# A third of the gate and value products of the last two units, from 28 half-block matmuls to 49 quarter-block matmuls

## Chip, cores and metric

One NeuronCore of one Trainium2 chip runs the whole program; the other seven stand idle. The metric is the device time of one execution in microseconds (us), the median of several. Engines are named as in the profile: PE is TensorE's matmul stream and PEld its weight loads, DVE is VectorE, ACT is ScalarE, POOL is GpSimd, SP is SyncE, which here issues nearly all DMAs.

## What is computed

Retention over 8 batches and 8 heads of 576 positions and 64 channels, then a gated feed-forward layer over the 4608 tokens that come out of it, all in float32:

```python
ret = scale * (q @ k.T) * Dmat                 # Dmat: decay gamma**(i-j), causal
x   = (ret @ v)                                # (8, 576, 8*64) -> (4608, 512)
xn  = x / sqrt(mean(x*x, -1) + 1e-6) * rms_g
g   = xn @ w_gate                              # 512 -> 1536
out = (g / (1 + exp(-g)) * (xn @ w_val)) @ w_out   # 1536 -> 512
```

## The kernel before, in words

**Units.** The tokens are cut into nine units of 512 tokens, numbered 0 to 8 in the code (`u`). Retention makes the rows of x for a unit; the feed-forward part then works on one unit at a time. Units 0 and 1 run in a first stage that also rounds the weights and builds their block sums (a written plan of steps sets its order). Units 2 to 8 run in the loop at L1342 to L1380. Retention for later units is worked in between the groups of units 2 to 6; units 7 and 8 have none beside them.

**Seven products for eight.** Every matrix product of units 2 to 8 is done by a Strassen-Winograd scheme: both operands are cut 2 x 2, seven block products replace eight, and sums of blocks are formed before (of x and of the weights) and after (of the results). `sums_of_x` (L615) makes the sums of x once per unit, `sums` and `t_of[u]` hold them. The seven weight blocks of each group lie ready in DRAM (`w_up_blocks`), as do those of the output weights (`w_out_blocks`).

**Gate and value groups.** `up(u, n)` (L697) makes one group n = 0 to 5; groups with even n are gates (`m` = 0), those with odd n the values that multiply them. Each block product is 256 x 256 by 256 tokens: four matmuls of 128 x 128 weights against 256 moving columns (L706), accumulated in one PSUM bank. A group is 28 matmuls and four banks (`x`, `y`, `z`, `w`). After a product an ACT copy (L732) or a DVE addition (L713) takes its bank; ACT then applies Silu (L727), or DVE multiplies into the gates (L725), and `differences` (L785) prepares operands of the output product.

**Output products.** `across(u)` (L843) multiplies the 1536 hidden rows by `w_out` with the scheme nested twice: 7 x 7 = 49 products of quarters, three matmuls each (one for each 128 rows of the contraction), 128 moving columns, 147 matmuls per unit (L876). `inner_sums` (L821) forms the four inner sums for each of the seven pieces, mostly on POOL; results gather in `vec`, the front part of the tile `vi`; the last step, `combine` (L1065), is seven additions of 128 x 4 x 128 on POOL. `store` (L1078) writes them out with eight DMAs of 128 KB.

**Weights on their way.** Each group's and each output piece's blocks pass through `ring`, a room of 17408 words per partition (L125). `pieces` lists them in order of use with their places (L640 on); a group takes 3584 words (1.84 MB), an output piece 2688 (1.38 MB). `refill` (L656) issues the next loads on SP's queue as soon as the place is free, and is called by `used` (L686) when the products of a piece have been issued. SP works strictly in order; a DMA that waits for room holds everything behind it.

**Order around the change.** The loop is a schedule by hand: each `yield` in `up` and `across` marks a product, and the loop places other work by (group, product):

```python
if n == 1 and i == 4:              # L1349
    store(u - 1)
if n == 2 * NG - 2 and i == 1:     # L1351: group 4
    inner_sums(u, 0, 0)
    inner_sums(u, 1, 0)
if more and i == 2 and 0 < n <= NHP:
    prepare(j0 + n); fetch(j0 + n + 1)   # retention: transposes, next loads
```

So on SP's queue the stores of unit u-1 stand in group 1 of unit u, behind the first `fetch` of that unit and before the other ones. `combine` of unit u-1 is issued at the end of `across(u - 1)`. The eight PSUM banks go round in order of use.

Of the kernel before, what the change touches and what calls it, by code (L numbers as in the profile page):

```python
# [10 lines left out]
F32 = mybir.dt.float32  # L11
U32 = mybir.dt.uint32
AF = mybir.ActivationFunctionType
# [31 lines left out]
def kernel(  # L45
# [32 lines left out]
    assert S == U + L and NU == B + 1 and NK == 3 and NG == 3  # L78

    const = ctx.enter_context(tc.tile_pool(name="const", bufs=1))  # L80
    raw = ctx.enter_context(tc.tile_pool(name="raw", bufs=1))
    att = ctx.enter_context(tc.tile_pool(name="att", bufs=2))
    xp = ctx.enter_context(tc.tile_pool(name="xp", bufs=3))
    tmp = ctx.enter_context(tc.tile_pool(name="tmp", bufs=4))
    PS = bass.MemoryType.PSUM
    dram = ctx.enter_context(tc.tile_pool(name="dram", bufs=1, space=bass.MemoryType.DRAM))
    banks = ctx.enter_context(tc.tile_pool(name="banks", bufs=8, space=PS))

    def bank(name):
        return banks.tile([P, 512], F32, tag="b", name=name)  # L90
# [4 lines left out]
    def row(name):  # L95
        return tmp.tile([P, U], F32, tag="n", name=name, bufs=3)
# [447 lines left out]
    def same_rows():  # L544

        t = tmp.tile([P, SQ], F32, tag="d", name="d", bufs=1)
        nc.vector.tensor_reduce(
            out=t, in_=ident.rearrange("p (a b) -> p b a", b=SQ), axis=mybir.AxisListType.X,
            op=ALU.add,
        )  # L550
        nc.vector.tensor_copy(
            out=alike.rearrange("p (a b) -> p a b", b=SQ),
            in_=t.unsqueeze(1).to_broadcast([P, P // SQ, SQ]),
        )
# [73 lines left out]

    UP, OUT = 7 * 2 * 2 * P, 7 * NK * P
    w_up_d = dram.tile([2 * NG, P, UP], F32, name="w_up_blocks")
    w_out_d = dram.tile([7, NK, P, 7 * P], F32, name="w_out_blocks")
    FIRST_ORDER = (A11, S4, A12, S1, S2, S3, A22)
# [7 lines left out]
    pieces = [("out", 0, n) for n in range(7)] + [("out", 1, n) for n in range(4, 7)]  # L642
    N_FIRST = len(pieces)
    for u in range(2, NU):
        pieces += [("up", u, n) for n in range(2 * NG)] + [("out", u, n) for n in range(7)]
    places = []
    at = AT_SUMS
    for kind, u, n in pieces:
        size = UP if kind == "up" else OUT
        if at + size > RING:  # L650
            at = AT_SETS if kind == "out" and u < 2 else 0
        places.append((at, at + size))
        at += size
    n_sent = n_used = 0

    def refill(most=len(pieces)):  # L656

        nonlocal n_sent
        while n_sent < min(most, len(pieces)):
            a, z = places[n_sent]  # L660
            kind, u, n = pieces[n_sent]
            if any(a < y and x < z for x, y in places[n_used:n_sent]):
                return
            if u > 1 and n_used < N_FIRST and a < NF * U:
                return
            o = ring[:, a:z]
            if kind == "up":
                src = w_up_d[n]
            else:
                o = o.rearrange("p (c x) -> p c x", c=NK)  # L670
                src = w_out_d[order_of(u)[n]].rearrange("c p x -> p c x")
            nc.sync.dma_start(out=o, in_=src)
            n_sent += 1

    def piece(kind, u, n):
        if kind == "out" and u == 1 and n < 4:
            i = pieces.index(("out", 0, n + 3))
        else:
            i = pieces.index((kind, u, n))
        assert i < n_sent and (i == n_used or kind == "out" and u == 0)  # L680
        a, z = places[i]
        if kind == "up":
            return ring[:, a:z].rearrange("p (b c f) -> p b c f", b=7, c=2)
        return ring[:, a:z].rearrange("p (c n d) -> p n c d", n=7, c=NK)

    def used():  # L686
# [10 lines left out]
    def up(u, n):  # L697


        m, f = n % 2, n // 2 * 2  # L700
        w = piece("up", u, n)

        def product(blk, ps, start):
            for i in range(2):
                for c in range(2):
                    nc.tensor.matmul(  # L706
                        ps[:, i * HU : i * HU + HU], lhsT=w[:, PLACE[blk], c, i * P : i * P + P],
                        rhs=t_of[u][blk][:, c], start=(start and i == c == 0), stop=False,
                        skip_group_check=True,
                    )  # L710

        def add(o, a, ps):
            nc.vector.tensor_tensor(out=o, in0=a, in1=pairs_of(ps), op=ALU.add)  # L713

        def result(f, t, nm, a, ps):

            o = h[:, f : f + 2, t * HU : t * HU + HU]
            c = pairs_of(ps)
            if a is not None:
                c = o  # L720
                if m:
                    c = pairs_of(temp(f"{nm}_{u}_{n}")) if nm == "c12" else a
                add(c, a, ps)
            if m:
                nc.vector.tensor_tensor(out=o, in0=o, in1=c, op=ALU.mult)  # L725
            else:
                nc.scalar.activation(out=o, in_=c, func=AF.Silu)  # L727

        x_, y, z, w_ = (bank(f"{nm}_{u}_{n}") for nm in "xyzw")
        s1, u2, u4 = (pairs_of(temp(f"{nm}_{u}_{n}")) for nm in ("m1", "u2", "u4"))  # L730
        product(A11, x_, True)
        nc.scalar.copy(out=s1, in_=pairs_of(x_))  # L732
        yield
        product(S2, y, True)
        add(u2, s1, y)
        yield
        product(S1, z, True)
        add(u4, u2, z)
        yield
        product(A12, x_, False)  # L740
        result(f, 0, "c11", None, x_)
        yield
        product(S3, w_, True)
        result(f + NH, 1, "c22", u4, w_)
        yield
        product(S4, z, False)
        result(f, 1, "c12", u2, z)
        yield
        product(A22, w_, False)
        used()  # L750
        result(f + NH, 0, "c21", u2, w_)
        if m:
            differences(u, f)
        yield

    def up_plain(u, k, n):
# [28 lines left out]
    def differences(u, f):  # L785

        hh = h_1 if u == 1 else h
        b11, b12, b22 = hh[:, f : f + 2, :HU], hh[:, f : f + 2, HU:], hh[:, NH + f : NH + f + 2, HU:]
        for o, a, b in ((t1_of(u)[:, f : f + 2], b12, b11), (b12, b22, b12)):
            nc.vector.tensor_tensor(out=o, in0=a, in1=b, op=ALU.subtract)  # L790
# [52 lines left out]
    def across(u):  # L843
# [148 lines left out]
        for n, nm in enumerate(banks_in_turn):  # L992
# [66 lines left out]
                if n in ahead:  # L1059
                    inner_sums(u, ahead[n])  # L1060
            yield
        if u and not last:
            combine(slice(0, 4), nc.gpsimd)

    def combine(b, eng=nc.vector, late=False):  # L1065

        t = vec[:, b] if isinstance(b, slice) else vec[:, b : b + 1]
        for o, x, y in (
            (A12, A11, A12), (A11, A11, S2), (S1, A11, S1), (S4, S1, S4), (A11, A11, S3),
            (S3, S1, S3), (A22, A11, A22),  # L1070
        ):
            eng.tensor_tensor(out=t[:, :, o], in0=t[:, :, x], in1=t[:, :, y], op=ALU.add)  # L1072
        if late:
            store(NU - 1, b)

# [263 lines left out]

    with tc.manual_schedule():  # L1342
        start()
        for u in range(2, NU):
            j0 = NHP * (u + 1)
            more = u + 1 < B
            for n in range(2 * NG):
                for i, _ in enumerate(up(u, n)):
                    if n == 1 and i == 4:  # L1349
                        store(u - 1)  # L1350
                    if n == 2 * NG - 2 and i == 1:  # L1351
                        inner_sums(u, 0, 0)
                        inner_sums(u, 1, 0)
                    if more and i == 2 and 0 < n <= NHP:
                        if j0 + n < len(jobs):
                            prepare(j0 + n)
                            fetch(j0 + n + 1)
                    if u + 1 < NU and n == 2 * NG - 1:
                        if i < NHP:
                            gather(u + 1, i, square(u + 1, i))  # L1360
                        elif i == NHP:
                            fold(u + 1)
                        elif i == 6:
                            meet(u + 1)
                    if (u, n, i) == (2, 2, 1):
                        same_rows()
                    if more and (n, i) == (NHP, 5) and j0 + NHP == len(jobs):
                        values(j0 + NHP - 1)
                if more and n <= NHP and (n or u == 2):
                    if j0 + n < len(jobs):  # L1370
                        slot(j0 + n, rest=(n > 0))
                    else:
                        carried(j0 + n - 1)
            for i, _ in enumerate(across(u)):
                if u + 1 == NU:
                    continue
                if i == 2:
                    root(u + 1)
                elif i in (3, 4, 5, 6):
                    scale_x(u + 1, (i - 3,))  # L1380
                elif i == 8:
                    sums_of_x(u + 1)
# [27 lines left out]
```

## Time and profile before

| | us |
|---|---|
| median of 3 executions (1100.55 to 1248.33) | 1101.38 |
| the profiled execution | 1099.84 |
| its span, first to last instruction | 1098.0 |
| granted TensorE clock over the span | 0.997 |
| unit 7, first gate matmul to the first of unit 8 | 882.6 to 988.2 |
| six gate and value groups of unit 7 | 72.5 |
| output products of unit 7 | 32.9 |

The profile gives, for each engine, the time in which it was busy and the number of instruction records; a float32 matmul leaves two records. The chain of work is followed back from the last instruction, at each step to what released it. A group of instructions is named by line, engine, operation and the tiles it writes and reads. A timeline lists instructions by start; in it, equal neighbours are merged (x8 is eight records) and lengths of matmuls overlap, since they are pipelined. A window view gives each engine's busy time in a stretch, then the clock, the share of the 16 DMA engines and GB/s. In units 2 to 5, which have retention beside them, a unit takes 115 to 116 us; DMA moves 220 to 250 GB/s there. In unit 7 it moves 214 GB/s, in unit 8 150.

### The profile page before, as it was taken

How to read it: one execution, taken by the hardware profiler on the slowest of the kernel's cores; microseconds unless marked ns; L12 is line 12 of the kernel's file. 1: busy time of each engine (PE TensorE's matmuls, PEld its weight loads, DVE VectorE, ACT ScalarE, POOL GpSimd, SP SyncE). 2: the span in 40 equal slices, each digit the busy share in tenths (PEclk: the TensorE clock that was granted, in tenths of full speed). 3: DMA queues.
4: the chain of work that ended last, by engine and by line, in shares of the span. 5: the costliest groups of instructions: out<-in, count | busy, mean ns of one | idle time of the engine just before them, and what ended most of it. 6: DMA issues, size and time to landing. Idle time of an engine off the chain costs nothing.

```text
span 1098.0 us, 24349 instructions
## 1 busy us (share of the span) xinstructions
PE 1085.8 (99%) x10006; PEld 911.3 (83%) x10006; DVE 729.9 (66%) x1299; ACT 328.2 (30%) x739; POOL 443.8 (40%) x421
## 2 busy tenths in 40 slices
PE   8899999999999999999999999999999999999998
PEld 7654444479988899889988998899888988998898
DVE  3778568877866774677667855677565735674467
ACT  6754565331123412332034203330233111201110
POOL 0026325538430195027702571238321932383236
PEclk9899999999999999999999999999999999999999
DMA  8847776696978876787678875988475755575471
GB/s 215 191 151 254 284 249 205 213 338 193 289 279 227 196 287 223 187 233 245 249 212 200 292 260 148 250 247 293 140 199 198 281 192 175 194 282 163 148 251 40
DMA packets 253871, 243.60 MB, mean 222 GB/s; under 512 B 193216, under 2 KB 213824, under 8 KB 247616
## 3 DMA queue, kind: packets, MB, share of 16 engines
q1 hardware_dynamic: 252320, 241.64, 69.8%
q8 instruction: 79, 1.29, 0.5%
q10 hardware_dynamic: 1440, 0.40, 0.2%
q14 instruction: 32, 0.26, 0.1%
HBM read 211.92 MB, written 30.08 MB: 220 GB/s over the span
## 4 chain that ended last, share of the span: by engine, by line
PE 97%; DVE 1%; ACT 1%; issue 1%; POOL 0%; POOLq 0%; DVEq 0%; ACTq 0%
PE up L766 15%; PE x L706 14%; PE w L706 13%; PE z L706 13%; PE y L706 7%; PE xo L876 6%; PE xp L876 4%; PE zo L876 4%; PE zp L876 3%; PE wo L876 2%; PE yo L876 2%; PE av L386 2%; PE wp L876 2%; PE av L406 2%; PE s L295 2%; PE yp L876 2%
## 5 line engine op out<-in xcount | busy, mean ns | idle before, releaser
L766 PE MATMUL up<-x,ring 128*128 128x512 f32 x384 | 167.1, 594 | 0.0
L706 PE MATMUL x<-x,ring 128*128 128x256 f32 x672 | 161.0, 382 | 0.0
L706 PE MATMUL w<-sums,ring 128*128 128x256 f32 x672 | 158.8, 379 | 0.0
L706 PE MATMUL z<-x,ring 128*128 128x256 f32 x672 | 158.7, 379 | 0.0
L828 POOL TENSOR_TENSOR vi<-h 128x384 f32<-128x384 f32 x32 | 42.4, 1327 | 274.2 <-DVE h L725 264.7
L766 PEld LDWEIGHTS up<-x,ring 128*128 128x128 f32 x384 | 72.2, 190 | 89.4 <-issue 85.1
L706 PEld LDWEIGHTS z<-x,ring 128*128 128x128 f32 x672 | 127.7, 190 | 17.4
L706 PEld LDWEIGHTS w<-sums,ring 128*128 128x128 f32 x672 | 127.6, 190 | 17.4
L706 PEld LDWEIGHTS x<-x,ring 128*128 128x128 f32 x672 | 125.3, 190 | 17.5 <-ACT m L732 0.2
L833 POOL TENSOR_TENSOR vi<-h 128x384 f32<-128x384 f32 (+2 forms) x46 | 43.9, 954 | 148.9 <-DVE h L725 148.9
L1072 POOL TENSOR_TENSOR vi<-vi 128x512 f32<-128x512 f32 (+1 forms) x77 | 78.2, 1029 | 52.0 <-DVE vi L903 35.5
L706 PE MATMUL y<-sums,ring 128*128 128x256 f32 x336 | 79.4, 379 | 0.0
L732 ACT COPY m<-x 128x512 f32<-128x512 f32 x42 | 24.6, 586 | 173.5 <-PE x L706 173.5
L713 DVE TENSOR_TENSOR h<-u,w 128x512 f32<-128x512 f32 x42 | 28.9, 687 | 67.7 <-PE w L706 67.7
L706 PEld LDWEIGHTS y<-sums,ring 128*128 128x128 f32 x336 | 63.8, 190 | 8.7
L713 DVE TENSOR_TENSOR u<-m,y 128x512 f32<-128x512 f32 x42 | 28.8, 685 | 59.9 <-PE y L706 59.3
L727 ACT ACTIVATE h<-h 128x512 f32<-128x512 f32 x63 | 39.7, 630 | 83.4 <-DVE h L713 83.4
L1192 POOL TENSOR_TENSOR vi<-vi 128x512 f32<-128x512 f32 (+1 forms) x24 | 40.7, 1697 | 30.7 <-DVE vi L1181 17.6
L713 DVE TENSOR_TENSOR u<-u,z 128x512 f32<-128x512 f32 x42 | 28.9, 687 | 32.7 <-PE z L706 32.6
L1192 POOL TENSOR_TENSOR ring<-ring 128x512 f32<-128x512 f32 x24 | 30.4, 1273 | 49.2 <-DMA w_up_blocks<-ring 43.7
L333 DVE SCALAR_TENSOR_TENSOR ret<-s,causal 128x256 f32<-128x256 f32 (+2 forms) x112 | 32.0, 336 | 22.3 <-PE s L295 22.3
L430 ACT COPY x<-av 128x192 f32<-128x192 f32 (+6 forms) x136 | 37.8, 278 | 27.9 <-PE av L406 26.5
(327 smaller groups left out, 2055.4 us busy)
## 6 DMA issues: line engine op xcount, KB each, us to landing
ring<-w_out_blocks SPq DMA_DIRECT2D x59, 1344.0 KB, 6.9
ring<-w_up_blocks SPq DMA_DIRECT2D x42, 1792.0 KB, 7.5
w_out_blocks<-vi SPq DMA_DIRECT2D x21, 448.0 KB, 6.3
out_dram<-vi SPq DMA_DIRECT2D x64, 128.0 KB, 3.0
qraw<-in_q_dram SPq DMA_DIRECT2D x96, 72.0 KB, 4.8
kraw<-in_k_dram SPq DMA_DIRECT2D x96, 72.0 KB, 2.6
k<-in_k_dram SPq DMA_DIRECT2D x48, 128.0 KB, 2.8
v<-in_v_dram SPq DMA_DIRECT2D x48, 128.0 KB, 2.8
```

What stands on the lines that cost most here:

```text
L333: nc.vector.scalar_tensor_tensor(out=ret[:p, e, a:z], in0=s[e][:p, a * L : z * L].rearrange("p (c k) -> p c k", k=L), scalar=float(_gamma( ...
L430: nc.scalar.copy(out=o, in_=part)
L706: nc.tensor.matmul(ps[:, i * HU : i * HU + HU], lhsT=w[:, PLACE[blk], c, i * P : i * P + P], rhs=t_of[u][blk][:, c], start=(start and i == ...
L713: nc.vector.tensor_tensor(out=o, in0=a, in1=pairs_of(ps), op=ALU.add)
L727: nc.scalar.activation(out=o, in_=c, func=AF.Silu)
L732: nc.scalar.copy(out=s1, in_=pairs_of(x_))
L766: nc.tensor.matmul(ps, lhsT=w[:, PLACE[blk], c % 2, i * P : i * P + P], rhs=x_of[u][:, c], start=(c == 0), stop=(c == NHP - 1),)
L828: eng.tensor_tensor(out=i1, in0=x12, in1=x11, op=ALU.subtract)
L833: eng.tensor_tensor(out=o[:, c], in0=a[:, c], in1=b[:, c], op=op)
L876: nc.tensor.matmul(ps, lhsT=lhs[:, c], rhs=w[:, s, c], start=((nm, s // 4) not in first), stop=False, skip_group_check=True,)
L1072: eng.tensor_tensor(out=t[:, :, o], in0=t[:, :, x], in1=t[:, :, y], op=ALU.add)
L1192: nc.gpsimd.tensor_tensor(out=t[o], in0=t[x], in1=t[y], op=op)
```

## The change

Three things change. First, in units 7 and 8 the groups 1, 2 and 3 (of 0 to 5) are made by a new function, `up_deep`, with the scheme nested twice, as the output products have it: each of the seven blocks is cut 2 x 2 again, so a group is 49 matmuls of 128 x 128 by 128 columns, in eight PSUM banks. The weight blocks' inner sums are made once, on POOL, by `inner_blocks` in units 3, 4 and 5 (group 1, 2 and 3 in turn), from the ring, and stored in DRAM by seven DMAs of 256 KB each. The ring takes each such group as two pieces (four blocks and three), old blocks and new sums side by side, 7168 words instead of 3584, by three DMAs a piece. The inner sums of x are made on DVE at the start of units 7 and 8 (`inner_x`). The results are summed on POOL (`combine_in`, seven additions of 128 x 4 x 128 a group) and finished (Silu, multiplication, differences) during the next group. The pools of the retention part are closed in unit 7 to make room.

Second, in units 3, 4 and 5 the stores of the unit before move from group 1 to the sixth group, behind the last retention loads of the unit; in units 7 and 8 to group 2. Third, `combine` of the unit before moves, for those units, from the end of `across` into the first group of the next unit: behind `inner_blocks`, or behind the second part of `inner_x`. In units 7 and 8 the two early inner sums move from group 4 to group 5.

```diff
+    HALVES = (0, 4), (4, 7)
+    DEEP = range(1, 4)
+    LATE = (NU - 2, NU - 1)
+    USED_IN = (A11, S2, S1, S3), (A12, S4, A22)
...
-        pieces += [("up", u, n) for n in range(2 * NG)] + [("out", u, n) for n in range(7)]
+        for n in range(2 * NG):
+            if u in LATE and n in DEEP:
+                pieces += [("in", u, (n, i)) for i in range(2)]
+            else:
+                pieces.append(("up", u, n))
+        pieces += [("out", u, n) for n in range(7)]
...
+            elif kind == "in":
+                i, z = HALVES[n[1]]
+                o = o.rearrange("p (b k x) -> p b k x", k=2, x=4 * P)
+                src = w_up_d[n[0]].rearrange("p (b x) -> p b x", b=7)
+                for x, y in spans_of(IN_ORDER[i:z]):
+                    nc.sync.dma_start(
+                        out=o[:, x : x + len(y), 0], in_=src[:, y[0] : y[0] + len(y)]
+                    )
+                src = w_in_d[n[0] - DEEP[0]].rearrange("p (b x) -> p b x", b=7)[:, i:z]
+                o = o[:, :, 1]
...
+    def up_deep(u, n):
...
+        def product(blk, nm, start):
+            half = int(blk in USED_IN[1])
+            w = piece("in", u, (n, half))[:, IN_ORDER.index(blk) - HALVES[half][0]]
+            if start:
+                held_in[nm] = bank(f"{nm}o_{u}_{n}"), bank(f"{nm}p_{u}_{n}")
+            for i, s in enumerate(PARTS):
+                nc.tensor.matmul(
+                    held_in[nm][i // 4][:, i % 4 * P : i % 4 * P + P], lhsT=w[:, IN_AT[s]],
+                    rhs=moving(blk, s), start=(start and i % 4 == 0), stop=False,
+                    skip_group_check=True,
+                )
+            if blk == USED_IN[half][-1]:
+                used()
...
+        product(A11, "x", True)
+        copy(first, "x")
+        yield
+        product(S2, "y", True)
+        add(first, first, "y")
...
-        if u and not last:
+        if u and not last and u + 1 not in LATE and u - 1 not in DEEP:
             combine(slice(0, 4), nc.gpsimd)
...
-                for i, _ in enumerate(up(u, n)):
-                    if n == 1 and i == 4:
+                deep = u in LATE and n in DEEP
+                for i, _ in enumerate((up_deep if deep else up)(u, n)):
+                    if (n, i) == (0, 0) and u - 2 in DEEP:
+                        inner_blocks(u, u - 2)
+                        combine(slice(0, 4), nc.gpsimd)
+                    if saves and (n, i) >= (0, 4):
+                        saves.pop(0)()
+                    if u in LATE and n == 0 and i in (0, 2):
+                        inner_x(u, i // 2)
+                        if i:
+                            combine(slice(0, 4), nc.gpsimd, after=last_x[0])
+                    if (n, i) == ((2 * NG - 1, 0) if u - 2 in DEEP else (1 + (u in LATE), 4)):
                         store(u - 1)
-                    if n == 2 * NG - 2 and i == 1:
+                    if (n, i) == ((2 * NG - 1, 2) if u in LATE else (2 * NG - 2, 1)):
                         inner_sums(u, 0, 0)
                         inner_sums(u, 1, 0)
...
+                    for _ in range(FINISH.get((n, i), 0) if u in LATE else 0):
+                        unfinished.pop(0)()
```

`FINISH` places what group 3 leaves over: its first multiplications at product 5 of group 4, the others at product 6, its differences at product 1 of group 5. Groups 1 and 2 are finished from within the next group, from the sixth and the fifth product on.

## The prediction

> **What bounds the kernel now.** I read the page's engine table and its chain first, to see whether any engine but TensorE sets the end.
>
> ```profile
> PE 1085.8 (99%) x10006; PEld 911.3 (83%) x10006; DVE 729.9 (66%) x1299; ACT 328.2 (30%) x739; POOL 443.8 (40%) x421
> PE 97%; DVE 1%; ACT 1%; issue 1%; POOL 0%; POOLq 0%; DVEq 0%; ACTq 0%
> ```
>
> 97% of the chain is TensorE, so the time moves by what TensorE's own work moves, plus any new hole in it. Next the timeline of PE alone, where the end of an output product meets the first gate group of unit 8. Columns: start, length, and at the end the number of records; each f32 matmul of the code leaves two records.
>
> ```profile
> 868.55 1.50 PE L876 MATMUL yo<-ring,h 128*128 128x128 f32 x12
> 869.89 0.83 PE L876 MATMUL yp<-ring,h 128*128 128x128 f32 x6
> 870.56 0.83 PE L876 MATMUL yo<-ring,vi 128*128 128x128 f32 x6
> 871.23 1.50 PE L876 MATMUL yp<-ring,vi 128*128 128x128 f32 x12
> 872.57 0.83 PE L876 MATMUL yo<-ring,vi 128*128 128x128 f32 x6
> 873.24 1.50 PE L876 MATMUL wo<-ring,h 128*128 128x128 f32 x12
> ...
> 882.62 1.89 PE L706 MATMUL x<-x,ring 128*128 128x256 f32 x8
> 884.35 1.89 PE L706 MATMUL y<-sums,ring 128*128 128x256 f32 x8
> ```
>
> Lengths overlap, so the pace is read from starts. With 128 moving columns 42 records go from 868.55 to 873.24: 111.67 ns each. With 256 columns eight go in 1.73 us; a whole group of 56 takes 12.09 us (next view), 215.9 ns each. Half the columns cost 52% of the time.
>
> Then the same stretches by window (PE, PEld, DVE, ACT, POOL, clock, DMA share, GB/s): one gate group, one unit's output products, and two stretches of 4 us in which the DMA queue had work all the time.
>
> ```profile
> 882.62:894.71 12.09, 12.09 (x58) 10.65 (x57) 3.90 (x6) 2.44 (x4) 8.80 (x7) 1.00 0.42 152
> 955.28:988.19 32.91, 32.91 (x297) 32.91 (x296) 24.98 (x33) 2.91 (x6) 27.80 (x25) 1.00 0.79 278
> 962.00:966.00 4.00, 4.00 (x39) 4.00 (x38) 3.76 (x9) 0.98 (x2) 3.84 (x5) 1.00 0.94 346
> 966.00:970.00 4.00, 4.00 (x39) 4.00 (x38) 1.04 (x2) 0.36 (x1) 3.84 (x5) 1.00 0.88 326
> ```
>
> PE is full, the clock is 1.00, and while a gate group runs DVE, ACT and DMA are mostly free; weights move at 326 to 346 GB/s when they are wanted. Last, what the helpers cost: the POOL timeline, the DVE timeline and the page's DMA issues.
>
> ```profile
> 870.64 1.32 POOL L833 TENSOR_TENSOR vi<-vi,h 128x384 f32<-128x384 f32 x1
> 874.74 1.00 POOL L833 TENSOR_TENSOR vi<-t 128x384 f32<-128x384 f32 x1
> 883.65 9.12 POOL L1072 TENSOR_TENSOR vi<-vi 128x512 f32<-128x512 f32 x7 [5.03 <-DVE vi L903]
> ```
>
> ```profile
> 871.03 1.48 DVE L625 TENSOR_TENSOR x<-x 128x512 f32<-128x512 f32 x1
> 878.13 0.69 DVE L903 TENSOR_TENSOR vi<-vi,wo 128x512 f32<-128x512 f32 x1 [0.38 <-PE wo L876]
> 878.74 0.55 DVE L903 TENSOR_TENSOR vi<-vi,wp 128x384 f32<-128x384 f32 x1
> ```
>
> ```profile
> ring<-w_up_blocks SPq DMA_DIRECT2D x42, 1792.0 KB, 7.5
> out_dram<-vi SPq DMA_DIRECT2D x64, 128.0 KB, 3.0
> ```
>
> **The change part by part.**
>
> TensorE. Six groups (1, 2 and 3 of units 7 and 8) lose 28 matmuls of 256 columns each: 6 x 56 x 215.9 ns = 72.5 us. They get 49 matmuls of 128 columns each: 6 x 98 x 111.67 ns = 65.7 us. That is 6.85 us less, all of it on the path. The row has the same shape (128x128 against 128x128, f32), so the pace is taken from it; the bounds are half of the wide record (108.0 ns, 63.5 us, 9.0 us gained) and the pace at which nothing is gained, 72.5 us / 588 = 123.3 ns, 10% over the row.
>
> The Trainium skill, TensorE: Matmul & The Clock Gate, section LDWEIGHTS, speaks against small moving blocks: a weight load costs by its columns, 107 ns for 128 of them, whatever streams past it. In the second window weight loads do fill all 32.91 us. By the page alone 588 loads would take 62.7 us as a floor; the row stands at 65.7 and decides.
>
> DVE. Each of the five additions per group becomes two, 0.69 + 0.55 us for 0.69: 2.75 us more a group. Eight additions per unit for quarters of x, four of 512 and four of 384 elements, cost 5.0 us at 0.69 and 0.55, and 10 us if all meet POOL as at 871.03. They stand in group 0, where DVE is busy 3.90 of 12.09, and are read first in group 1. A deep group holds 6.2 us of additions and at most 4.1 us of multiplications and differences (6 x 0.69): 10.3 of its 10.95 us. On the path: nothing, while DVE gets each bank read before its product comes round again, three products (4.7 us) later. If that cover is gone, PE waits for the bank.
>
> ACT copies two halves twice instead of one block once, about 1.6 us more a group; it has 9 us idle.
>
> POOL. Each deep group adds seven additions of 512: 9.1 us (the 883.65 row), 55 us in all. POOL idles in these groups once the last unit's seven are done; per deep group 9.1 fits into 10.95. Gates and values are ready about 10.6 us after a group's end, and the code asks for them at the sixth product of the next group, 9.4 to 10.4 us after it, behind an addition that ends near 10.8. A wait of a microsecond on DVE or ACT is covered by the same 4.7 us. The two early inner sums that move from group 4 to group 5 need only the first results: POOL starts them when group 5 starts and needs 6.1 us (five to six such instructions took 926.8 to 932.9 before), and the next ones wait for group 5 until 7.8 us anyway.
>
> New blocks in units 3 to 5: per unit four POOL instructions of 768 elements and four of 128. From 1.30 us per 512 and 0.46 to 0.91 us per 128 that is 10 to 11 us, ahead of the seven additions of the unit before. POOL was idle from 892.8 to 926.8 there, so these end by 28 us into the unit, and nothing reads the outputs before the stores in group 5. Seven stores of 256 KB, 1.84 MB, take 5.4 us at 340 GB/s. They stand on SP's queue ahead of one weight load and the first retention loads of the unit; SP may wait for POOL to 17 us, while that weight load is wanted at 48 us (group 4) and the retention loads were issued at 18.7 us before as well. Cost nothing.
>
> Stores of outputs. The eight stores go from group 1 past four sets of retention loads and four or five weight loads to group 5. Issued there they need about 6.3 us on SP and 3.0 us to land, some 10 us into the group (12.09 us long); the first copy into that room follows 21 matmuls of 0.223 us, at 16.8 us, and PE needs the bank it frees two such pieces into the output stage, at 21.5 us. Nothing, with 6 to 11 us of spare. Where they stood no wait of PE is shown, so the move gains nothing either.
>
> Weights. A deep group loads 3.67 MB instead of 1.84. The ring is 17408 words; from the places I worked out when a piece may start (its room is released) and when it is wanted. Tightest is unit 8: from the end of group 0, at 12.1 us, 2.10 MB must land by 23.0, 5.77 MB by 34.0, 7.34 by 40.2 and 9.18 MB (with group 4's) by 44.9. Taking 2.4 us of fixed latency (a 32 KB load's landing), 9.18 MB in 32.8 us ask for 302 GB/s. At 326 the piece has 2.2 us to spare; at 280 it is 2.4 us late; at 244 it is 7.2 us late and the gain is gone. The new pieces move in runs of 2 KB, which no row shows alone; the nearest, runs of 3.5 KB, are the two windows above. I take 0.5 us (a piece or two just late, as at 297 GB/s), bounds 0 and 6.9.
>
> Sum: -6.85 + 0.5 = -6.35 us. The profiled execution took 1099.84 us (span 1098.0), 1.5 under the median of 1101.38; from it the sum gives 1093.5, from the median 1095.0. I forecast 1095.0.
>
> The second rule that speaks against it is SBUF — State Buffer, section Who interferes with whom: a VectorE instruction with two SBUF inputs and a reading GpSimd instruction take turns, whole instruction by instruction. The trace agrees (1.48 for 0.69 on DVE, 1.32 for 1.00 on POOL). By the rule alone 9.1 + 4.1 us would have to fit into 10.95, and POOL would fall 2.3 us behind in each deep group.
>
> **The rivals.**
>
> POOL late. If the deep sums take 12 to 14 us instead of 9.1 (the 1.32-fold of the row above, all the time), DVE and ACT stand at the results of one group while the next group's banks wait. For it: in the output stage POOL is busy 27.80 of 32.91 us. Against: most DVE additions here read PSUM, and at 0.69 and 0.55 they show no contention. It takes 1 to 3 us per unit: 1096 to 1101.
>
> Weights late. At 250 to 290 GB/s the pieces of unit 8 come 1.3 to 6.3 us late: 1096 to 1101. For it: short runs. Against: 326 and 346 with 3.5 KB runs.
>
> Slower than before. The same ring, but below 244 GB/s, decides the sign: at 200 GB/s unit 8 is 45.9 + 2.4 - 32.8 = 15.5 us late and unit 7 (5.51 MB between 18.3 and 44.9 us) 3.4 us: 1094.5 + 18.9 = 1113. For 2% it would take 29 us, some 175 GB/s. Against: the 128 KB stores in runs of 512 bytes are the only slow row, and they are slow by their issue (8.9 us for eight).
>
> It does not do what it says: records that go to another PSUM place each time pace at 118 to 123 ns, and 49 products cost as much as 28: 1098 to 1101.5. Against: output products change place every six records without a step in the starts.
>
> **How the numbers follow.** Full gain with 0 to 1.5 us of waits (1094 to 1096.5) 0.70; weights late 0.11; POOL late 0.09; no gain by pace 0.05; slower 0.05. The likeliest gives 1095. The low end is the half-record bound, 1092.4, rounded to 1092.5; the high end, 1100.0, leaves out the slower rival and the upper parts of three others, under 2 in 10. 2%, about what a measurement of this kernel tells from no change, is 22 us: nothing here gains as much (0.01), and only the ring below 175 GB/s loses as much (0.02).
>
> **What would show it.** Right: deep records start every 111 to 112 ns, six groups of 10.95 us, DMA at 290 to 350 GB/s in units 7 and 8, no idle time before them. Wrong: idle PE before the first deep record of a half, released by a DMA into the ring (weights late); idle before a product, released by DVE or ACT (POOL late); an output stage of units 3 to 5 longer than 33 us (stores); a record pace over 113 ns.

## The result, and the profile after

| us | before | after |
|---|---|---|
| median of all executions | 1101.38 | 1093.01 |
| the profiled execution | 1099.84 | 1092.38 |
| its span | 1098.0 | 1090.6 |
| first matmul of unit 2 (end of the first stage) | 305.11 | 304.71 |
| units 2 to 6 | 577.51 | 577.52 |
| unit 7 | 105.58 | 102.20 |
| unit 8, gate and value groups | 72.52 | 69.14 |
| the rest (unit 8's output stage) | 37.24 | 37.02 |

The ratio is 0.9917, 95% interval 0.9892 to 0.9943; here and below the ratio need not be the quotient of the two medians. Of the five executions of before one (1248.33) was disturbed and is left out of it; the other four took 1100.42, 1100.55, 1101.38 and 1105.80. The change was measured twice more, beside the experiments: 1092.35 against 1098.62 and 1090.94 against 1098.86 (below). The table is read from the first gate matmul of each unit in PE's timeline. Units 7 and 8 lost 3.38 us each, 6.76 together, and units 2 to 6 nothing. The other 0.6 us lie in the first stage and the last output stage, which run the same code; the first stage also ended at 301.7 to 306.2 in the experiments, so that part is scatter (the last section has more on it).

The engine table and the chain of after:

```profile
PE 1079.2 (99%) x10258; PEld 913.4 (84%) x10258; DVE 758.9 (70%) x1345; ACT 337.0 (31%) x757; POOL 529.7 (49%) x487
...
PE 96%; DVE 1%; ACT 1%; DMA 1%; issue 1%; SPq 0%; POOL 0%; POOLq 0%; DVEq 0%; ACTq 0%
```

TensorE has 252 records more (6 x 42) and is busy 6.6 us less. The helpers do more: POOL 86 us, DVE 29. The PE timeline of after, at the start of the three deep groups of unit 8 and of the first plain group behind them:

```profile
996.52 0.61 PE L881 MATMUL xo<-x,ring 128*128 128x128 f32 x4
996.96 0.61 PE L881 MATMUL xo<-inner_x,ring 128*128 128x128 f32 x4
...
1029.40 1.89 PE L744 MATMUL x<-x,ring 128*128 128x256 f32 x8
```

294 records go from 996.52 to 1029.40: 111.8 ns each, and no line between them carries an idle time. The windows of after, group by group (PE, PEld, DVE, ACT, POOL, clock, DMA share, GB/s):

```profile
984.43:996.52 12.09, 12.09 (x59) 10.64 (x57) 8.54 (x14) 2.45 (x4) 3.61 (x3) 1.00 0.76 264
996.52:1007.47 10.95, 10.95 (x100) 10.95 (x99) 6.07 (x10) 2.55 (x5) 5.23 (x5) 1.00 0.64 213
1007.47:1018.42 10.95, 10.95 (x101) 10.95 (x100) 6.47 (x12) 2.13 (x4) 8.82 (x7) 1.00 0.92 309
1018.42:1029.40 10.98, 10.98 (x101) 10.98 (x99) 10.72 (x16) 2.13 (x4) 9.06 (x7) 1.00 0.97 318
```

A deep group takes 10.95 us for 12.09. PE and its weight loads are both full, and in the third group DVE (10.72) and DMA (0.97) nearly are too: there is little room left for the helpers. POOL's timeline shows the sums of results:

```profile
1008.36 9.14 POOL L910 TENSOR_TENSOR deep_c<-deep_c 128x512 f32<-128x512 f32 x7 [6.46 <-DVE deep_c L902]
1020.03 19.53 POOL L910 TENSOR_TENSOR deep_c<-deep_c 128x512 f32<-128x512 f32 x14 [2.53 <-DVE deep_c L902]
```

SP's timeline around unit 8, with the loads of deep pieces (inner sums at L708, plain blocks at L700; 1013.46 is group 4's load):

```profile
986.35 0.36 SPq L708 DMA_DIRECT2D ring<-w_in_blocks  x1
991.53 2.06 SPq L700 DMA_DIRECT2D ring<-w_up_blocks  x2
996.71 0.36 SPq L708 DMA_DIRECT2D ring<-w_in_blocks  x1
...
1013.46 0.33 SPq L708 DMA_DIRECT2D ring<-w_up_blocks  x1
1013.88 8.98 SPq L1299 DMA_DIRECT2D out_dram<-vi  x8
```

The first line matters: a load into the room of unit 8's group 0 goes out at 986.35, when that group, which runs to 996.52, has just ended its first product. The last block of this load lies on the first block of group 0 in the ring, and the load went out when that block was read: it waited for the blocks beneath it, not for the whole piece.

### The profile page after: what moved, and what is told of

It reads as the page before. It is cut to its first block, busy times and chain, and to the rows that moved or that the text cites. A ratio compares the mean times of both kernels' runs of the same rounds, so it can differ in the third digit from the quotient of the medians.

```text
span 1090.6 us, 25131 instructions
## 1 busy us (share of the span) xinstructions
PE 1079.2 (99%) x10258; PEld 913.4 (84%) x10258; DVE 758.9 (70%) x1345; ACT 337.0 (31%) x757; POOL 529.7 (49%) x487
## 4 chain that ended last, share of the span: by engine, by line
PE 96%; DVE 1%; ACT 1%; DMA 1%; issue 1%; SPq 0%; POOL 0%; POOLq 0%; DVEq 0%; ACTq 0%
PE up L977 15%; PE x L744 12%; PE w L744 11%; PE z L744 11%; PE xo L1087 6%; PE y L744 6%; PE xp L1087 4%; PE zo L1087 4%; PE zp L1087 3%; PE wo L1087 2%; PE yo L1087 2%; PE av L387 2%; PE wp L1087 2%; PE s L296 2%; PE av L407 2%; PE yp L1087 2%
## 5 line engine op out<-in xcount | busy, mean ns | idle before, releaser
L744 PE MATMUL x<-x,ring 128*128 128x256 f32 x576 | 138.4, 383 | 0.0
L744 PE MATMUL w<-sums,ring 128*128 128x256 f32 x576 | 136.2, 379 | 0.0
L744 PE MATMUL z<-x,ring 128*128 128x256 f32 x576 | 136.1, 379 | 0.0
L744 PEld LDWEIGHTS z<-x,ring 128*128 128x128 f32 x576 | 109.4, 190 | 14.9
L744 PEld LDWEIGHTS w<-sums,ring 128*128 128x128 f32 x576 | 109.4, 190 | 14.9
L744 PEld LDWEIGHTS x<-x,ring 128*128 128x128 f32 x576 | 106.9, 190 | 14.9 <-ACT m L770 0.2
L744 PE MATMUL y<-sums,ring 128*128 128x256 f32 x288 | 68.0, 379 | 0.0
L910 POOL TENSOR_TENSOR deep_c<-deep_c 128x512 f32<-128x512 f32 x42 | 55.5, 1335 | 19.9 <-DVE deep_c L902 11.5
L744 PEld LDWEIGHTS y<-sums,ring 128*128 128x128 f32 x288 | 54.7, 190 | 7.4
L1044 POOL TENSOR_TENSOR vi<-h,vi 128x384 f32<-128x384 f32 (+2 forms) x46 | 45.5, 989 | 3.6
```

The costliest lines, as they stand in the source:

```text
L744: nc.tensor.matmul(ps[:, i * HU : i * HU + HU], lhsT=w[:, PLACE[blk], c, i * P : i * P + P], rhs=t_of[u][blk][:, c], start=(start and i == ...
L910: nc.gpsimd.tensor_tensor(out=c[:, which, at(o)], in0=c[:, which, at(x)], in1=c[:, which, at(y)], op=ALU.add,)
L1044: eng.tensor_tensor(out=o[:, c], in0=a[:, c], in1=b[:, c], op=op)
```

## Experiments

All ratios are to the kernel before on the same chip. The kernel before took 1099.39 us beside the first four, 1098.62 beside the change again, group 0, group 4 and the late saves, and 1098.86 beside the other three.

**The move of the stores alone.** The kernel before, with one line changed:

```diff
-                    if n == 1 and i == 4:
+                    if (n, i) == ((5, 0) if u in (3, 4, 5) else (1, 4)):
```

> The kernel before, with only the stores of outputs moved in units 3, 4 and 5 from group 1 to the sixth group. Theory A (all of the gain is the shorter stream of matmuls, 6 groups x 1.13 us): 0, so 1100 to 1102 us, units 2 to 6 as long as before (577.5 us from the first gate matmul of unit 2 to that of unit 7, within 0.2). Rival B (the gain beyond 6.8 us comes from the queue order): 0.5 to 2 us faster, and units 3 to 5 shorter.

Measured: 1099.18 us, ratio 0.9997 (0.9986 to 1.0008). By itself the move is worth nothing that can be measured.

**The change without that move.** The stores go back to group 1:

```diff
-  if (n, i) == ((2 * NG - 1, 0) if u - 2 in DEEP else (1 + (u in LATE), 4)):
+  if (n, i) == (1 + (u in LATE), 4):
```

> The changed kernel, with the stores of units 3 to 5 back in group 1, where they wait on SP's queue for POOL's sums, which come later now (20 to 28 us into the unit instead of 10). Theory A: as the changed kernel, 1092 to 1094, because the loads behind the stores have over 20 us to spare. Rival B: 1 to 4 us slower, with a hole before retention's matmuls or before the weights of group 4 in units 3 to 5.

Measured: 1099.23 us, ratio 0.999 (0.9976 to 1.0005): nearly the whole gain is gone. (It is not gone in every execution: three of the twelve took 1094.2 to 1095.7, the others 1098.5 to 1101.1.) Group 0 and the deep groups take 44.95 us, as in the change. The loss of the profiled execution is in unit 4 (1.1 us), unit 5 (4.8 us) and unit 6 (0.6 us). SP's timeline in unit 5, which begins at 653.84:

```profile
668.26 0.80 SPq L828 DMA_DIRECT2D w_in_blocks<-vi  x2
...
672.72 7.98 SPq L166 DMA_DIRECT2D qraw<-in_q_dram  x4
...
686.91 0.54 SPq L828 DMA_DIRECT2D w_in_blocks<-inner  x1
687.55 5.23 SPq L1299 DMA_DIRECT2D out_dram<-vi  x8
...
693.52 4.74 SPq L166 DMA_DIRECT2D qraw<-in_q_dram  x4
```

The same queue in the change, whose unit 5 begins at 652.24:

```profile
671.11 6.63 SPq L166 DMA_DIRECT2D qraw<-in_q_dram  x4
...
684.02 0.54 SPq L828 DMA_DIRECT2D w_in_blocks<-inner  x1
684.66 0.38 SPq L708 DMA_DIRECT2D ring<-w_up_blocks  x1
685.69 5.08 SPq L166 DMA_DIRECT2D qraw<-in_q_dram  x4
```

And in the kernel before, whose unit 5 begins at 652.63:

```profile
671.50 2.06 SPq L165 DMA_DIRECT2D qraw<-in_q_dram  x4
...
678.68 6.33 SPq L1085 DMA_DIRECT2D out_dram<-vi  x8
...
686.02 4.21 SPq L165 DMA_DIRECT2D qraw<-in_q_dram  x4
```

With the saves ahead of them the first retention loads take 13 to 14 us to issue (671.11 to 683.9 in the change; in the kernel before 7 us, 671.50 to 678.6). With the eight stores behind those, the second set of loads starts 39.7 us into the unit instead of 33.4. Their transposes then stand ahead of a bank's addition in DVE's order (the first two lines below; the third is the addition, the fourth the matmul that waits for the bank):

```profile
704.31 0.78 DVE L268 STREAM_TRANSPOSE qT<-qraw 128x576 f32<-128x576 f32 x1 [3.25 <-ACT qraw L263]
706.43 0.78 DVE L268 STREAM_TRANSPOSE kT<-kraw 128x576 f32<-128x576 f32 x1 [1.34 <-DMA kraw<-in_k_dram]
707.71 0.67 DVE L751 TENSOR_TENSOR u<-u,w 128x512 f32<-128x512 f32 x1
...
708.43 2.82 PE L744 MATMUL w<-sums,ring 128*128 128x256 f32 x8 [2.92 <-DVE u L751]
```

Of the 4.8 us in unit 5 the wait is 2.9; the rest is nearly all the clock behind it (last section).

**Unit 8 only.**

```diff
-    LATE = (NU - 2, NU - 1)
+    LATE = (NU - 1,)
```

> The changed kernel with nested products in unit 8 alone. Theory A: half of the gain, 3.4 us: 1097 to 1098, unit 7's six gate and value groups back at 72.5 us, unit 8's at 69.1. Rival B: more than half of the gain stays, since all helpers and moved stores of units 3 to 5 stay: under 1096.

Measured: 1097.25 us, ratio 0.9982 (0.9972 to 0.9992). In the profile unit 7 takes what it took (72.66 us of groups) and unit 8's groups 69.14, 3.4 less. The medians give 2.1 (0.9 to 3.1); the profile's 3.4 lies just outside that interval, and what the difference comes from is not shown.

**A smaller ring in units 7 and 8.** 12288 words of the 17408:

```diff
-        if at + size > RING:
+        if at + size > (12288 if u in LATE else RING):
```

> The changed kernel with only 12288 of the ring's 17408 words used in units 7 and 8, so that weights can be fetched less far ahead. Theory of the prediction (a piece's loads start only when every old piece under it is used up; the ring is within 2 us of starving): about 11 us slower than the changed kernel, 1104. Rival (the loads start block by block as soon as the words under them are read; 7 us to spare in the full ring): about 8 us slower, 1101. If the ring's size does not matter: 1093.

Measured: 1093.15 us, ratio 0.9938 (0.992 to 0.9956). The theory and its rival both missed; it is as if the ring's size did not matter. Group 0 and the deep groups of unit 8 take 44.96 us, as in the change:

```profile
982.13:1027.09 44.96, 44.96 (x352) 43.51 (x351) 31.78 (x50) 9.25 (x17) 26.70 (x21) 1.00 0.87 319
```

What the smaller ring takes is spare time. The weights of group 4 were issued at 1013.46 and landed at 1022.31 in the change, 7.1 us ahead of their first matmul at 1029.40; here they were issued at 1019.09 and landed at 1026.50, 0.6 us ahead of 1027.09.

**The change again:**

> The change itself once more, on the same chip as the three kernels beside it, to measure them against. TensorE theory: two stages of three deep groups at 10.95 us in place of 12.1 make 6.9 us less; the profile showed 6.75 of it in units 7 and 8 and nothing anywhere else, so the median stands 6 to 8 us below the kernel before (ratio 0.9930 to 0.9945). Rival: the 8.4 us that the two first medians lay apart hold a gain outside the deep groups; then the ratio is below 0.993 and units 1 to 6 are shorter by over 1 us.

Measured: 1092.35 us, ratio 0.9951 (0.9934 to 0.9968), 6.3 us less. Units 2 to 6 take 577.80 us, units 7 and 8 what they took above.

**Group 0 too.** The inner sums of x move into the output stage before:

```diff
-    DEEP = range(1, 4)
+    DEEP = range(0, 4)
...
-                    if u in LATE and n == 0 and i in (0, 2):
-                        inner_x(u, i // 2)
-                        if i:
+                    if u in LATE and (n, i) == (0, 2):
...
+                elif i in (12, 13) and u + 1 in LATE:
+                    inner_x(u + 1, i - 12)
```

> Group 0 of units 7 and 8 goes in 49 products too, and the inner sums of x are made in the output stage of the unit before. TensorE theory: two more deep groups, each 56 times 215.9 ns against 98 times 111.7 ns, 1.14 us less, so 2.3 us below the change and 9 below the kernel before. Rival, VectorE: the 5 to 10 us of inner sums of x now lie behind the last outputs of the unit before and ahead of its first bank additions; if TensorE waits at the start of the unit for these sums or for a bank, 1 us or more for each unit is given back and the time is level with the change.

Measured: 1099.8 us, ratio 1.0004 (0.9993 to 1.0015). Units 7 and 8 gain 0.5 us each in place of 1.14, since the first deep group runs into the late sums of x (0.57 us from one record to the next for 0.11, behind DVE; some 0.2 us more were not traced). But unit 2 loses 7.46 us, a place that neither theory had named. There POOL now makes the inner sums of group 0 from the first moment, while DVE adds outputs of unit 1. The DVE timeline, then lines of ACT's and PE's:

```profile
305.73 7.92 DVE L1110 TENSOR_TENSOR vi<-vi 128x896 f32<-128x896 f32 x3
```

```profile
313.74 0.59 ACT L1102 COPY vi<-zo 128x512 f32<-128x512 f32 x1 [16.47 <-DVE vi L1110]
...
314.60 0.60 ACT L770 COPY m<-x 128x512 f32<-128x512 f32 x1
...
315.25 3.78 PE L744 MATMUL x<-x,ring 128*128 128x256 f32 x8 [4.66 <-ACT m L770]
```

Three additions take 7.92 us; in the change they take 3.09:

```profile
305.20 3.09 DVE L1110 TENSOR_TENSOR vi<-vi 128x896 f32<-128x896 f32 x3
```

ACT's copies of the last outputs wait for them, its copy of the gate bank (`m`) stands behind those, and TensorE behind that copy.

**Group 0 too, with POOL held off** until those additions are through; added to the kernel of the last run:

```diff
-    def inner_blocks(u, n):
+    def inner_blocks(u, n, after=None):
...
+                if after is not None:
+                    follow(step, after)
+                    after = None
...
-                        inner_blocks(u, u - 2)
+                        inner_blocks(u, u - 2, last_add[0] if u == 2 else None)
```

`last_add` is the latest DVE addition to the outputs.

> Group 0 in 49 products as in the run before, but the first inner sum of w of unit 2 waits for VectorE's last addition to the outputs of unit 1. Theory, taking turns: in the run before, three VectorE additions of the outputs took 7.92 us in place of 3.09 while GpSimd's inner sums of group 0 ran from the first moment of unit 2, ScalarE's copy of a bank and TensorE stood behind them, and that was the whole 7.46 us of unit 2; with GpSimd kept off until they are through, unit 2 takes what it takes in the change, and what stays is the 0.5 us that the late stage gains in each of units 7 and 8: 0.5 to 1.5 us below the change. Rival: the ring or SyncE held unit 2, since group 0's weights now have a second reader at the head of the unit; then unit 2 stays 5 us or more too long and the time is near the kernel before.

Measured: 1091.81 us, ratio 0.9935 (0.9922 to 0.9949). Unit 2's groups are back at 83.92 us, and the DVE timeline shows why:

```profile
304.86 3.08 DVE L1113 TENSOR_TENSOR vi<-vi 128x896 f32<-128x896 f32 x3
```

The profile gains 0.5 us in each of units 7 and 8 and loses 0.4 in the last output stage; the median is not below that of the change on the same chip (1090.94). So the overlap of POOL's inner sums with DVE's additions is shown as the cause of the 7.46 us. That the two take turns at a port is one way to read it and was not tested by itself. What group 0 gains is too little to measure.

**Group 4 too**, its inner sums of w made in unit 6:

```diff
-    DEEP = range(1, 4)
+    DEEP = range(1, 5)
...
+                    if (u, n, i) == (6, 1, 0):
+                        inner_blocks(u, u - 2)
```

> Group 4 of units 7 and 8 goes in 49 products too (its inner sums of w are made in unit 6). TensorE theory: 2.3 us below the change. Rival, GpSimd: the inner combination of a deep group takes it 9.1 us and stands ahead of its inner sums of the output stage, which it makes one after the other with 1.2 us to spare at the last in unit 7 of the kernel before; then TensorE waits in the output stages of units 7 and 8 for some 5 us each, and the time is 1 to 8 us above the change.

Measured: 1107.48 us, ratio 1.0082 (1.0057 to 1.0107), 15 us above the change: the rival, larger than expected. POOL in unit 7 (the change ends its sums of results at 937.4 and begins its inner sums at 939.20):

```profile
924.34 28.94 POOL L910 TENSOR_TENSOR deep_c<-deep_c 128x512 f32<-128x512 f32 x25
953.24 1.00 POOL L1039 TENSOR_TENSOR vi<-h 128x384 f32<-128x384 f32 x1
```

POOL comes 14 us later to the output stage, which takes 40.5 us for 32.9, and 47.7 for 37.0 in unit 8. The wait in unit 7 (in unit 8 one of 7.4 us stands for the same releaser):

```profile
960.55 2.50 PE L1087 MATMUL xp<-ring,vi 128*128 128x128 f32 x10 [4.42 <-POOL vi L1044]
```

The rival had priced the waits alone, at some 5 us a unit. Behind each of them 6.2 us of TensorE's work ran at half the granted clock, which adds about 3.1 us a unit to the profiled execution.

**The saves moved behind the loads, stores in group 1**, to tell the two things ahead of the second loads apart:

```diff
-                    if saves and (n, i) >= (0, 4):
+                    if saves and (n, i) >= (2, 4):
...
+                    if (n, i) == (1 + (u in LATE), 4):
```

> The change with the stores of outputs of units 3 to 5 back in group 1, as in the slower run before, but with the seven saves of inner sums of w begun in group 2, behind the loads of retention, in place of group 0. Theory, the order on SyncE: with the saves ahead of them the first loads of retention take 14 us to issue in place of 7, and the 8 stores then push the second loads to 40 us into the unit, so bank additions wait behind late transposes on VectorE; with the saves gone from there the second loads start at 33 us as before and the time is that of the change, 6 to 8 us below the kernel before. Rival, GpSimd: the sums of the outputs stand behind 10 us of inner sums of w, so the stores wait for them wherever the saves are; then units 4 and 5 stay 1 and 5 us long and the time is level with the kernel before.

Measured: 1095.75 us, ratio 0.9975 (0.9957 to 0.9992): part of the loss is made good. Each against the kernel before on its chip, the change gains 6.3 us by the medians, this run 2.9 and the run without the move 0.2; in units 4 and 5 of the profiles 2.8 of the 5.9 us are left. SP's timeline in unit 5, which begins at 651.45:

```profile
670.32 1.95 SPq L166 DMA_DIRECT2D qraw<-in_q_dram  x4
...
677.38 5.73 SPq L1299 DMA_DIRECT2D out_dram<-vi  x8
...
685.09 3.03 SPq L166 DMA_DIRECT2D qraw<-in_q_dram  x4
...
696.62 1.07 SPq L828 DMA_DIRECT2D w_in_blocks<-vi  x2
```

The second loads start 33.6 us into the unit, as the theory said, and the wait of 2.9 us is gone. A hole of about 1.1 us is left in each of units 4 and 5: in unit 5 TensorE waits for ACT's `tick` of the retention part, in unit 4 the profile names no releaser. The saves now stand ahead of the third loads. Not all of this need be the saves' doing: the profile of the change's third measurement, below, has a hole of 0.5 us before a matmul of the same line and tiles in unit 6, also without a releaser.

**Inner sums alone.** The kernel before with POOL's inner sums of w in units 3 to 5, but no saves and no nested products (`LATE = ()`, stores in group 1, `saves.extend` taken out):

> The kernel before with the inner sums of w added on GpSimd in units 3 to 5 and nothing else: no saves, no nested products, the stores of outputs at their old place in group 1. It tells what the residue of the run with the saves late was. Theory, the queue on SyncE: the sums on GpSimd end by 28 us into the unit, nothing of SyncE stands behind the saves any more, and the time is that of the kernel before within 1 us. Rival, GpSimd's lateness: the sums of the outputs, and with them the stores and the second loads of retention, come 10 us later, and units 4 and 5 are 1 us or more longer each, 2 to 6 us in all.

Measured: 1100.03 us, ratio 1.0006 (0.9995 to 1.0018). The 10 us of POOL ahead of the outputs' sums cost nothing that can be measured. The saves alone, in group 0 with the stores late, cost units 3 to 5 nothing either (the change itself), and the stores alone cost nothing (the kernel before). So what the run without the move lost came from saves and stores together, in SP's queue ahead of the second loads. Whether the holes that the late saves leave come from the third loads was not tried and stays open.

**The change a third time**, beside the inner sums alone and group 0 with POOL held off:

> The change once more, to measure the two kernels beside it against on one chip: 6 to 8 us below the kernel before.

Measured: 1090.94 us, ratio 0.9932 (0.9917 to 0.9946), 7.9 us less. The 6.76 us of the profile lie within the intervals of all three measurements.

## Why the prediction was right or wrong

**TensorE: right.** Forecast 6.85 us, measured 6.76: the pace of the output products held for the new ones (111.8 against 111.67 ns). No idle time and no rise at the change of PSUM places showed, so the rival by pace falls. An estimate from the Trainium skill (TensorE: Matmul & The Clock Gate, section LDWEIGHTS: 107 ns for a weight load of 128 columns) puts the floor of the six groups at 62.7 us; they took 65.7, with PEld full.

**The waits in the ring: the term of the sum that was mis-sized, 0.5 us forecast, 0.1 measured** (no idle time stands before a deep record; 0.1 is all that lies between 6.85 and 6.76). The step that failed is "when a piece may start (its room is released)". It was worked out by whole pieces, so that unit 8's loads were to begin at the end of group 0. But loads start block by block, 10 us before the piece above them is done: five of the six loads of group 2, 2.88 MB of the 9.18, were issued by 993.26 and had landed by 996.58, and group 0 ended at 996.52. The rate was low too, but that did not decide: by the prediction's own 326 GB/s and 2.4 us the 1.84 MB of group 4, issued at 1013.46, would land at 1021.5, and they landed at 1022.31. Over unit 8's group 0 and deep groups the page of transfers shows slices (1.1 us each) of 404 to 410 GB/s while runs of 2 KB move, and the 8 us from 1004.93 moved 377 GB/s; in its rows of loads the last number is the median time to landing:

```profile
GB/s 304 295 384 313 391 222 56 251 226 188 0 87 309 404 146 0 60 262 410 410 408 209 388 404 404 75 206 280 382 357 255 234 334 324 324 150 331 421 446 347
...
ring<-w_in_blocks SPq DMA_DIRECT2D x2, 1024.0 KB, 6.5
...
ring<-w_up_blocks SPq DMA_DIRECT2D x2, 512.0 KB, 3.9
```

Instead of 2.2 us there are 7.1 us of spare, and a ring smaller by 29% still leaves 0.6. The rival "weights late" was far off, and so was "slower". The sign "DMA at 290 to 350 GB/s in units 7 and 8" did not come: unit 7 moved 262 and unit 8 218 (its groups 279).

**The stores: true of the kernel before, wrong for the change.** "... the move gains nothing either" holds for the kernel before, and the run of the move alone shows it. In the change the same move is worth about 6 us, and that the change has it is luck as far as the prediction goes. But "Cost nothing" for the saves holds only because the stores had left that place: with saves in group 0 and stores in group 1, 6 us are lost. The two edits were priced one by one, each against the old order of SP's queue; together they queue. The bound was in reach: the prediction let SP stand to 17 us and put 1.84 MB of saves ahead of the loads, but it did not add the stores' 5 us to that and ask when the second loads come.

**DVE and POOL: right.** The inner sums of x added 4.6 us to group 0 (8.5 for 3.9), a little under the 5 to 10 that were forecast; seven sums of results took 9.14 to 9.8 us for 9.1, and those of the first deep group were ready 10.0 us after its end for 10.6. Contention shows in single rows, not in the sum. The rival "POOL late" is real one group further: with group 4 too it costs 15 us.

**"2%, about what a measurement of this kernel tells from no change": wrong.** The intervals reach 0.11 to 0.26% to either side, 1 to 3 us. A gain of 6.4 us on 1101, 0.6%, was forecast and could be told from none. The 0.97 that the prediction leaves for a change under 2% is borne out, but a change under 2% is not one that cannot be seen. The step took the one execution of 1248.33 for the scatter; the other two lay 0.8 us apart, and of the two taken since one stands beside them and one 4.4 us above.

**The base and the low end: too high.** "... from the median 1095.0. I forecast 1095.0" is the second step that failed. The result, 1093.01, stands 2.0 us under it. From the profiled execution the sum gave 1093.5, and that execution took 1092.38: 0.4 us of the difference are the waits, 0.6 the scatter in the unchanged parts. The median of three as the base added 1.5, and the median of after lies 0.6 above its profiled execution. Before took 1098.6 to 1099.4 beside the experiments, where it was measured often; from there the same sum gives 1092.3 to 1093.0. The low end, 1092.5, was the bound of the records' pace set off from the same base, with nothing for the base itself. The first ratio, 0.9917, is 9.1 us on 1101.38, more than that bound of 9.0, though TensorE gained 6.76: the surplus lies in the scatter of the two measurements, of before's 1105.80 above all, and the later pairs of medians give 6.3 and 7.9.

## What to carry to other kernels

Replacing TensorE work by cheaper TensorE work paid here by the pace of a row of the same shape, as long as every helper fitted beside it; how near the next group is to breaking that is read from the fullest helper window (here DVE 10.72 and POOL 9.06 of 10.98), and one group too many cost twice the gain. Edits that share an in-order queue are priced together: list what stands ahead of each DMA that somebody waits for, after the whole change. And before a class of result is forecast, the resolution is taken from how close the executions lie, an outlier such as 1248.33 set aside.

## What the hardware showed that was not expected

**A hole in TensorE costs more than its length.** After the 4.7 us of idle time in unit 2 of the run with group 0, the granted clock fell, and the next matmuls took twice as long (window: PE, clock, DMA share, GB/s):

```profile
310.00:315.20 5.20, 0.59 (x3) 0.85 1.01 430
315.20:320.50 5.30, 5.25 (x12) 0.50 0.41 164
320.50:325.00 4.50, 4.50 (x25) 1.00 0.01 2
```

Twelve records in 5.2 us are 0.43 us each for 0.216: 2.6 us on top of the 4.7, which is all but 0.2 of the 7.46. The 4.4 us of the run with group 4 did the same:

```profile
960.50:963.00 2.50, 2.45 (x11) 0.50 0.00 0
```

The hole of 2.9 us in the run without the move left 0.68 over the next 2.9 us and 0.83 over the 4.7 after them; that of 1.1 us in unit 4 of the run with the saves late left 1.00. In the clock records of the profiles the half clock lasts 3.41 us after the hole of 2.9, 6.83 in all around those of 4.4 and 4.7, and 10.24 around that of 7.4: one, two and three times the same length. The Trainium skill, TensorE: Matmul & The Clock Gate, section What's actually happening, says that the clock halves after an idle window of some 3.4 us and comes back after as long a busy one. The lengths agree with it, but 2.9 us without work were enough here.

The same stretches make part of the scatter. Counted in lengths of 3.41 us and without the first 7 us of the span, the first stage ended at 301.7 and 302.5 in the two profiles with no such stretch in it, at 304.0 to 304.8 with one, at 304.4 to 305.3 with two and at 305.2 and 306.2 with three. The profiles of before and after have two each.

**VectorE and GpSimd side by side.** Three DVE additions with both inputs in SBUF took 2.64 us each beside POOL's inner sums and 1.03 without; POOL's took 2.4 to 2.5 us each there and 1.81 in the change. The Trainium skill, SBUF — State Buffer, section Who interferes with whom, says that such a pair contends for a shared read port, which is an exclusive lock. If they take turns by whole instructions, one turn of each, 1.81 + 1.03, would be 2.84; the rows stand a little under it, so they agree nearly. In the deep groups this cost nothing on the path; most DVE additions there have one input in PSUM.
